# Weight chunks loaded in turns with batch 1, five shared buffers for k, q and v, and one compact copy, in a fused attention and MLP kernel

## The chip, the cores and the metric

The kernel runs on one core of one Trainium2 chip. The metric is the device time of one execution in microseconds (us); lower is better. A run of this one-core program is called slow when it is over 1.5% above the fastest run of the same kernel, and such runs are left out of ratios. The profile is one execution with the hardware profiler on; its span is a little shorter than the device time. All times inside a profile are counted from the start of its span.

Four engines matter here: TensorE (PE) multiplies matrices into the memory PSUM; ScalarE (ACT) and VectorE (DVE) empty PSUM, which is called an eviction; POOL and SyncE (SP) mostly issue DMA transfers. The granted clock is the share of its full speed that TensorE was given. A "dip" or "half clock" is a stretch of some 3.5 us in which it was near a half, so that four output matmuls take 1.90 us instead of 1.03.

## The reference, cut to what matters

```python
# q, k, v: (8 batches, 8 heads, 576 rows, 64); p: (8, 8, 32, 64)
p_packed = softmax(p @ k.T / 8) @ v            # 32 packed rows per head
attn     = softmax(q @ p_packed.T / 8) @ p_packed
x   = attn laid out as (8 * 576, 512)
h   = x @ w_in                                 # 512 -> 2048
g   = s * relu(h) ** 2 + b
out = g @ w_out                                # 2048 -> 512
```

## The kernel before

Everything is computed per batch. The packed values are first multiplied with W_in (`pw`, four chunks of 512 columns), so that a hidden block is the attention weights `aT` times `pw`, two by two matmuls of 288 columns. A block goes through a relu on ScalarE and a square on VectorE into `gT`; an output tile of 128 rows is then 16 "steps", one matmul with 128x512 of W_out each. `fill(n)` runs the next n output steps of the previous batch between other work, so that TensorE has something to do while ScalarE and VectorE empty PSUM.

Batches 0 to 2 transpose k and q on TensorE. From batch 3 on that is done by DMA from SyncE's queue: `dma_k` straight from the loaded k, `dma_q` from a copy of q re-laid by VectorE.

```python
def load(store, src, b, tag, h0=0, h1=H):          # POOL's queue, fp32 to bf16
    if h0 == 0:
        store[b] = rawp.tile([R, H, NC * D], BF16, tag=tag, name=tag)   # one buffer per tag
    pool.dma_start(out=store[b][:, h0:h1, :], in_=src[b, h0:h1]...)

for ch in range(NCH): load_w_in(ch)                # all of W_in, then all of W_out,
for m in range(0, NFF, 4): load_w_out(m, m + 4)    # then batch 1
load(kn, k, 1, "kn"); load(qn, q, 1, "qn"); load(vn, v, 1, "vn"); load_p(2, B)

def dma_k(b):                                      # SyncE's queue
    sp.dma_start_transpose(out=kT[b % 2]..., in_=kn[b]...)
def order_q(b):                                    # VectorE
    qr[b] = attp.tile(..., tag="qr", name="qr"); by_chunk(qr[b], qn[b])
def dma_q(b):                                      # SyncE's queue
    sp.dma_start_transpose(out=qT[b % 2]..., in_=qr[b]...)

# ... batches 0 and 1 by hand ...
second_scores(2); m1(1, 15)
todo = outs(1)                                     # five output tiles, 80 steps
packed_w1(2, 0); fill(6); weights(2, 0); fill(4); packed_w1(2, 1); weights(2, 1)
fill(6); packed_w1(2, 2); fill(4)
dma_k(3)

for b in range(2, B):                              # a = b + 1, c = b + 2
    # at block 1 (b == 2): packed_w1(2, 3), order_q(3), dma_q(3)
    # at block 3 + ...: first_scores(a), packed(a), second_scores(a) at block 9 (b == 2), ...
    # at block 4 (b == 2): loads(c)
    per = len(todo)
    for m in range(NFF):
        mlp_in(b, m)                               # one hidden block
        ... the steps of block m ...
        fill(per)
    fill(NFF * (NT + 1))
# [cut: the rest of the schedule]
```

The softmax here doesn't subtract the row's maximum and nothing guards it: scores larger than these inputs give would overflow.

Of the kernel before, what the change touches and what calls it, by code (L numbers as in the profile page):

```python
# [8 lines left out]
BF16 = mybir.dt.bfloat16  # L9
# [5 lines left out]
def kernel(  # L15
# [21 lines left out]
    B, H, S, D = q.shape  # L37
    NP = p.shape[2]
    DM = H * D
# [4 lines left out]
    R = 96  # L44
# [12 lines left out]

    constp = ctx.enter_context(tc.tile_pool(name="constp", bufs=1))
    wpool = ctx.enter_context(tc.tile_pool(name="wpool", bufs=1))
    rawp = ctx.enter_context(tc.tile_pool(name="rawp", bufs=1))  # L60
    attp = ctx.enter_context(tc.tile_pool(name="attp", bufs=1))
    atp = ctx.enter_context(tc.tile_pool(name="atp", bufs=2))
    smp = ctx.enter_context(tc.tile_pool(name="smp", bufs=2))
# [22 lines left out]
    def big(dt=F32):  # L86
        w = NB if dt == F32 else 2 * NB
        return psh.tile([P, 2, w], dt, tag="h", name="hps")


    kn, qn, vn = {}, {}, {}

    def load(store, src, b, tag, h0=0, h1=H):
        if h0 == 0:
            store[b] = rawp.tile([R, H, NC * D], BF16, tag=tag, name=tag)
        pool.dma_start(
            out=store[b][:, h0:h1, :],
            in_=src[b, h0:h1].rearrange("h (r c) d -> r h (c d)", c=NC),
        )
# [17 lines left out]
    def load_w_out(m0, m1):  # L117
        pool.dma_start(
            out=w_out_sb[:, m0:m1, :],
            in_=moe_w_out[m0 * P:m1 * P, :].rearrange("(m p) d -> p m d", p=P),  # L120
        )
# [17 lines left out]
    bvec = constp.tile([P, 1], F32, name="bvec")  # L139
    sp.dma_start(out=bvec[:], in_=moe_b[0:1].unsqueeze(0).to_broadcast([P, 1]))  # L140
    nc.scalar.preload_act_table_set("natural_log_exp_and_others")
    for ch in range(NCH):
        load_w_in(ch)
    for m in range(0, NFF, 4):
        load_w_out(m, m + 4)

    KW = H * HS + 32
    kT = [constp.tile([P, KW], BF16, name=f"kT{i}") for i in range(2)]
# [17 lines left out]
    def idle(n):  # L166

        t = big()
        for x in range(n):
            mm(t[:, 0, :], zeros[:, 0:P], zeros[:], start=True, stop=True)  # L170

    load(kn, k, 1, "kn")
    load(qn, q, 1, "qn")
    load(vn, v, 1, "vn")
    load_p(2, B)

# [24 lines left out]
    def prep_k(b, half):  # L201

        i = b % 2
        tp = big(BF16)
        for h4 in range(4):
            for cp in range(CP):
                tr(
                    tp[:, h4 // 2, (h4 % 2) * HS + cp * R:(h4 % 2) * HS + (cp + 1) * R],
                    kn[b][:, 4 * half + h4, cp * P:(cp + 1) * P],
                    identb[0:R, 0:R],  # L210
                )
        vec.tensor_copy(
            out=kT[i][:, half * 4 * HS:(half + 1) * 4 * HS].rearrange("p (a s) -> p a s", a=2),
            in_=tp[:, :, 0:2 * HS],
        )
# [5 lines left out]
        )  # L221

    def order_v(b):
        vr[b] = attp.tile([R, NC, HP, 2, D], BF16, tag="vr", name="vr")
        by_chunk(vr[b], vn[b])

    def order_q(b):
        qr[b] = attp.tile([R, NC, HP, 2, D], BF16, tag="qr", name="qr")
        by_chunk(qr[b], qn[b])

    def prep_q(b, half):

        i = b % 2
        tp = big(BF16)
        for x in range(2):
            hp = 2 * half + x
            for c in range(NC):
                for h2 in range(2):
                    tr(
                        tp[D * h2:D * h2 + D, x, c * R:(c + 1) * R],  # L240
                        qn[b][:, hp + HP * h2, c * D:(c + 1) * D],
                        identb[0:R, 0:R],
                    )
        for x in range(2):
            dst = qT[i][:, :, 2 * half + x, :]
            src = tp[:, x, 0:S].rearrange("p (c r) -> p c r", c=NC)
            if x == 0:
                act.copy(out=dst, in_=src)
            else:
                vec.tensor_copy(out=dst, in_=src)  # L250
# [34 lines left out]
    def packed(b, qd):  # L285
        i = b % 2
        if qd == 0:
            pps[b] = big()
        pp = pps[b]
        for hp in range(2 * qd, 2 * qd + 2):  # L290
            for c in range(NC):
                if b < N_PE_T:
                    for h2 in range(2):
                        o = hp * 2 * NP + h2 * NP
                        mm(
                            pp[D * h2:D * h2 + D, 0, o:o + NP],
                            vn[b][:, hp + HP * h2, c * D:(c + 1) * D],
                            e1[b][:, h2, c, hp, :],
                            start=(c == 0),
                            stop=(c == NC - 1),  # L300
                            tile_position=(0, D * h2),
                        )
                else:
                    mm(
                        pp[:, 0, hp * 2 * NP:(hp + 1) * 2 * NP],
                        vr[b][:, c, hp, :, :],
                        e1[b][:, :, c, hp, :],
                        start=(c == 0),
                        stop=(c == NC - 1),
                    )  # L310
        for c in range(NC):
            mm(
                pp[:, 1, qd:qd + 1],
                e1[b][:, qd, c, :, :],
                ones1[0:R, :],
                start=(c == 0),
                stop=(c == NC - 1),
            )
        if qd == NQ - 1:
            for h2 in range(2):  # L320
                vec.tensor_copy(
                    out=ppc[i][D * h2:D * h2 + D, :, :],
                    in_=pp[D * h2:D * h2 + D, 0, 0:HP * 2 * NP].rearrange("p (a j) -> p a j", a=HP)[
                        :, :, NP * h2:NP * h2 + NP
                    ],
                )
            rd[b] = smp.tile([P, NQ], F32, tag="rd", name="rd")
            vec.reciprocal(out=rd[b][:], in_=pp[:, 1, 0:NQ])
            rs[b] = smp.tile([P, NQ], F32, tag="rs", name="rs")
            vec.tensor_scalar_mul(out=rs[b][:], in0=rd[b][:], scalar1=scale)  # L330
# [63 lines left out]
    def packed_w1(b, ch, on_act=True):  # L394

        i = b % 2
        if ch == 0:
            pw[b] = ppw.tile([P, NQ, DFF], BF16, tag="pw", name="pw")
        t = big()
        packed_mm(i, ch, [t[:, qd, :] for qd in range(NQ)])  # L400
        dst = pw[b][:, :, ch * NB:(ch + 1) * NB]
        if on_act:
            act.activation(out=dst[:, 0], in_=t[:, 0, :], func=AF.Copy, scale=rd[b][:, 0:1])
        else:
            vec.tensor_scalar_mul(out=dst[:, 0], in0=t[:, 0, :], scalar1=rd[b][:, 0:1])
        vec.tensor_scalar_mul(out=dst[:, 1], in0=t[:, 1, :], scalar1=rd[b][:, 1:2])
# [33 lines left out]
    def bias_part(cps, m):  # L440
        mm(cps, onesb[:], w_out_sb[:, m, :], start=(m == 0), stop=(m == NFF - 1))
        if m == NFF - 1:
            vec.tensor_scalar_mul(out=biasrep[:], in0=cps, scalar1=bvec[:])
# [64 lines left out]
    def loads(b):  # L508
        load(kn, k, b, "kn")
        load(qn, q, b, "qn")  # L510
        load(vn, v, b, "vn")

    def m1(b, *ms):
        for m in ms:
            mlp_in(b, m)
# [20 lines left out]
    idle(3)  # L536
    weights(0, 0)
    weights(0, 1)
    packed_w1(0, 1, on_act=False)
    idle(6)  # L540
    m1(0, 0, 1, 2, 3)
    packed_w1(0, 2, on_act=False)
    m1(0, 4, 5, 6)

    todo = outs(0)
    first, second = todo[0], todo[1]
    bps = big()
    m = 7
    for m0 in range(0, NFF, 4):
        for x in range(m0, m0 + 4):  # L550
            bias_part(bps[:, 0, :], x)
        if m < NFF:
            m1(0, m)
        first.step(4)
        if m < NFF:
            m1(0, m + 1)
        second.step(4)
        if m < NFF:
            m1(0, m + 2)
        if m0 == 0:  # L560
            packed_w1(0, 3, on_act=False)
        m += 3
    loads(2)
    todo = todo[2:]

    def fill(n):
        run_outs(todo, n)

    prep_k(1, 0)
    prep_k(1, 1)  # L570
    fill(4)
    first_scores(1, 0)
    fill(4)
    first_scores(1, 1)
    fill(4)
    prep_q(1, 0)
    prep_q(1, 1)
    fill(4)
    packed(1, 0)
    packed(1, 1)  # L580
    twice_p(2, B)
    fill(5)
    packed_w1(1, 0)
    second_scores(1)
    fill(3)
    packed_w1(1, 1)
    weights(1, 0)
    fill(2)
    weights(1, 1)
    prep_p(2)  # L590
    fill(2)
    packed_w1(1, 2)
    prep_k(2, 0)
    m1(1, 0, 1)
    packed_w1(1, 3)
    m1(1, 2)
    prep_k(2, 1)
    m1(1, 3, 4)
    first_scores(2, 0)
    m1(1, 5, 6)  # L600
    fill(4)
    first_scores(2, 1)
    m1(1, 7, 8)
    prep_q(2, 0)
    prep_q(2, 1)
    m1(1, 9, 10)
    packed(2, 0)
    m1(1, 11)
    packed(2, 1)
    loads(3)  # L610
    m1(1, 12, 13, 14)
    second_scores(2)
    m1(1, 15)
    todo = outs(1)
    packed_w1(2, 0)
    fill(6)
    weights(2, 0)
    fill(4)
    packed_w1(2, 1)
    weights(2, 1)  # L620
    fill(6)
    packed_w1(2, 2)
    fill(4)
    dma_k(3)

    for b in range(2, B):
        a = b + 1
# [66 lines left out]
```

## Time and profile before

| what | value |
|---|---|
| device time, 3 runs | 270.11 us median (268.8 to 270.27) |
| span of the profile | 267.1 us |
| TensorE busy | 247.3 us, 93% |
| TensorE's longest wait | 2.07 us, for the transpose of batch 3's k |
| mean granted clock | 0.994 |

The prediction below shows the page, the waits and the timeline around that wait (start, duration, engine or queue, operation, with the idle time before and what ended it in brackets). Here is the timeline of SyncE's queue from 86 to 91 us (start, duration of the issue, queue, operation):

```profile
84.16 3.23 SPq L82 DMA_TRANSPOSE kT<-kn  x1
87.58 3.00 SPq L82 DMA_TRANSPOSE qT<-qr  x1
```

And POOL's timeline from 86 to 96 us, with what ended the idle time in brackets:

```profile
90.64 0.78 POOL L82 DMA_DIRECT2D kn<-in_k_dram  x1 [16.87 <-issue]
91.41 0.77 POOL L82 DMA_DIRECT2D qn<-in_q_dram  x1
92.17 0.77 POOL L82 DMA_DIRECT2D vn<-in_v_dram  x1
```

The reader is to see the order: batch 3's k transpose at 84.16, its q transpose at 87.58, and only then, from 90.64, the three loads of batch 4. The q transpose landed 5.0 us after its issue, at 92.6, 2.0 us after the first load was issued. Why the loads were that late: batch 4's k goes into the buffer from which batch 3's k transpose reads. The trace names no releaser for this one load (`issue`), but that transpose landed at 84.16 + 5.4 = 89.6 and the load was issued 1.1 us later; in the changed kernel the two times are 80.59 + 5.3 = 85.9 and 86.99, again 1.1 us apart; and the k loads of batches 5 and 6, at 113.25 and 134.19, wait for `DMA kT<-kn` by name.

### The profile page before, as it was taken

The page shows a single profiled execution, that of the slowest core. Times are in us where ns is not written, and L with a number is a line of the kernel's source. Part 1 is how long each engine was busy: PE and PEld are TensorE (multiplying, and loading weights), DVE is VectorE, ACT ScalarE, POOL GpSimd, SP SyncE. Part 2 cuts the span into 40 slices and gives each one's busy share as a digit, 9 for nine tenths or more (in the row PEclk, how much of TensorE's full clock was granted, in tenths as well). Part 3 has the DMA queues.
Part 4 walks back from the last instruction along what each step waited for, and adds up shares of the span by engine and source line. Part 5 has one row for each costly group of instructions (what it writes and reads, how often), then busy time and mean ns, then how long its engine had stood idle before and what let it go on. Part 6 is the DMA issues. An engine that isn't in the chain of part 4 may idle for free.

```text
span 267.1 us, 5619 instructions
## 1 busy us (share of the span) xinstructions
PE 247.3 (93%) x2312; PEld 139.5 (52%) x2348; DVE 146.4 (55%) x304; ACT 142.9 (53%) x217; POOL 29.3 (11%) x44
## 2 busy tenths in 40 slices
PE   7898899968989699899999999999999999999993
PEld 2544455636744365465556555665565555555441
DVE  2347456457657555765793459456944574444221
ACT  1337542387796347865855575548653773443000
POOL 8435001201100300030030012000000000000000
PEclk9999999999999799999999999999999999999999
DMA  7999999993893997699979869994731113111332
GB/s 75 198 202 206 206 203 164 145 194 37 131 143 75 157 201 151 115 150 235 169 94 182 203 128 164 140 212 79 134 87 42 39 42 81 39 39 42 79 79 79
DMA packets 54634, 34.32 MB, mean 128 GB/s; under 512 B 27472, under 2 KB 50000, under 8 KB 54608
## 3 DMA queue, kind: packets, MB, share of 16 engines
q0 software_dynamic: 25200, 18.61, 48.8%
q1 hardware_dynamic: 29408, 15.34, 26.6%
q8 instruction: 18, 0.29, 0.5%
q14 instruction: 8, 0.07, 0.1%
HBM read 37.23 MB, written 9.44 MB: 175 GB/s over the span
## 4 chain that ended last, share of the span: by engine, by line
PE 73%; DMA 11%; ACT 6%; DVE 4%; issue 3%; POOL 1%; DVEq 0%; POOLq 0%; ACTq 0%
PE yps L71 42%; PE hps L71 30%; DMA w_out_sb<-in_moe_w_out_dram 5%; DMA w_in_sb<-in_moe_w_in_dram 4%; ACT rlu L82 3%; DMA kT<-kn 2%; DVE pw L82 1%; PE hps L74 1%; ACT rcd L82 1%; ACT ld L82 1%; DVE ysb L82 1%; ACT pw L82 1%; DVE qr L82 1%; DVE gT L82 1%; POOL kn L82 1%
## 5 line engine op out<-in xcount | busy, mean ns | idle before, releaser
L71 PE MATMUL yps<-w_out_sb,gT 128*128 128x512 bf16 x544 | 138.1, 381 | 2.8 <-issue 1.6
L82 ACT ACTIVATE rlu<-hps 128x576 bf16<-128x576 f32 x128 | 82.4, 649 | 75.5 <-PE hps L71 68.0
L82 DVE TENSOR_TENSOR gT<-rlu 128x576 bf16<-128x576 bf16 x128 | 58.0, 456 | 73.0 <-ACT rlu L82 72.0
L71 PE MATMUL hps<-aT,pw 128*128 128x288 bf16 x512 | 83.3, 287 | 4.0 <-DVE pbd L82 1.7
L71 PEld LDWEIGHTS <-gT 128*128 128x128 bf16 x576 | 53.0, 98 | 50.5 <-issue 6.4
L71 PEld LDWEIGHTS <-pw 128*128 128x128 bf16 x512 | 49.5, 98 | 38.8 <-issue 5.1
L82 DVE SCALAR_TENSOR_TENSOR ysb<-yps,svec,biasrep 128x512 f32<-128x512 f32 x36 | 26.8, 747 | 14.3 <-PE yps L71 14.0
L82 DVE TENSOR_SCALAR pw<-hps,rd 128x512 bf16<-128x512 f32 (+1 forms) x26 | 24.4, 950 | 3.8 <-ACT pw L82 2.0
L82 ACT ACTIVATE e<-hps 96x768 bf16<-96x768 f32 x16 | 12.8, 802 | 15.7 <-PE hps L71 15.5
L82 ACT ACTIVATE pw<-hps,rd 128x1024 bf16<-128x1024 f32 (+1 forms) x18 | 16.6, 922 | 4.0 <-PE hps L71 3.9
L82 POOL DMA_DIRECT2D kn<-in_k_dram x9 | 6.9, 768 | 104.7 <-DMA kT<-kn 57.8
L82 DVE TENSOR_TENSOR aT<-e,rcd 128x576 bf16<-128x576 bf16 x16 | 12.1, 759 | 9.9 <-ACT rcd L82 9.9
L71 PE MATMUL hps<-w_in_sb,ppc 64*32 64x512 bf16 x256 | 12.3, 383 | 1.6 <-ACT e L82 0.4
L71 PE MATMUL hps<-zeros 128*128 128x512 bf16 x41 | 12.3, 427 | 1.4 <-DVE zeros L82 1.3
L82 ACT ACTIVATE e<-hps,rs 128x576 bf16<-128x576 f32 x16 | 10.9, 738 | 3.7 <-PE hps L71 3.7
L71 PE MATMUL hps<-pbd,kT 128*128 128x64 bf16 x192 | 8.9, 197 | 3.1 <-DMA kT<-kn 2.1
L82 ACT ACTIVATE rcd<-ld 128x576 f32<-128x576 f32 x16 | 10.9, 682 | 0.5
L71 PEld LDWEIGHTS <-kT 128*128 128x128 bf16 x192 | 8.1, 100 | 5.5 <-DMA kT<-kn 2.4
L82 ACT ACTIVATE ld<-hps 128x576 f32<-128x576 f32 x16 | 10.3, 643 | 0.9 <-PE hps L71 0.9
L71 PEld LDWEIGHTS <-ppc 64*32 64x32 bf16 x384 | 4.4, 89 | 10.4 <-issue 8.7
L82 POOL DMA_DIRECT2D qn<-in_q_dram x8 | 6.2, 775 | 13.5 <-PE hps L74 9.6
L71 PEld LDWEIGHTS <-zeros 128*128 128x128 bf16 x44 | 4.1, 106 | 6.3 <-issue 2.6
(45 smaller groups left out, 114.5 us busy)
## 6 DMA issues: line engine op xcount, KB each, us to landing
qn<-in_q_dram POOLq DMA_DIRECT2D x8, 576.0 KB, 10.8
vn<-in_v_dram POOLq DMA_DIRECT2D x8, 576.0 KB, 12.7
out_dram<-ysb SPq DMA_DIRECT2D x24, 192.0 KB, 2.3
kn<-in_k_dram POOLq DMA_DIRECT2D x7, 576.0 KB, 7.9
out_dram<-ysb SPq DMA_DIRECT2D x24, 128.0 KB, 2.5
w_in_sb<-in_moe_w_in_dram POOLq DMA_DIRECT2D x8, 256.0 KB, 12.9
w_out_sb<-in_moe_w_out_dram POOLq DMA_DIRECT2D x4, 512.0 KB, 13.4
out_dram<-ysb SPq DMA_DIRECT2D x24, 64.0 KB, 2.1
```

Source lines behind the costliest of these rows:

```text
L71: return tc.keep_in_program_order(nc.tensor.matmul(*a, **kw))
L74: return tc.keep_in_program_order(nc.tensor.transpose(*a, **kw))
L82: return lambda *a, **kw: tc.keep_in_program_order(f(*a, **kw))
```

## The change

The intent: W_in and W_out chunks load in turns with batch 1's tensors between them, so that output steps of batch 0 and the transposes of batch 1 can start while weights still arrive; freed filler is spread over batch 1; k, q, v and their re-laid copies share five rotating buffers, so that loads can be issued earlier; and the packed values leave PSUM in one copy of 128 partitions in place of two of 64.

```diff
-    rawp = ctx.enter_context(tc.tile_pool(name="rawp", bufs=1))
+    rawp = ctx.enter_context(tc.tile_pool(name="rawp", bufs=5))
+    def raw(name):
+        return rawp.tile([R, S // R * DM], BF16, tag="raw", name=name)[:]
... load(), order_q() and order_v() take their tile from raw() ...
-    for ch in range(NCH):
+    for ch in range(2):
         load_w_in(ch)
-    for m in range(0, NFF, 4):
-        load_w_out(m, m + 4)
+        load_w_out(4 * ch, 4 * ch + 4)
     load(kn, k, 1, "kn")
+    load_w_in(2)
+    load_w_out(8, 12)
     load(qn, q, 1, "qn")
+    load_w_in(3)
+    load_w_out(12, 16)
     load(vn, v, 1, "vn")
... packed(), b < N_PE_T: both halves of the heads into the same columns, then
+                vec.tensor_copy(out=ppc[i][:].rearrange("p a j -> p (a j)"), in_=pp[:, 0, 0:HP * NP])
... batch 0: six dummy matmuls (idle(6)) dropped; m1(0, ..) in turns with t0.step(2),
... t1.step(2), prep_k(1, ..), first_scores(1, ..), prep_q(1, ..); 16 fewer fills ...
... batch 1: fills of 5, 4, 3, 4 and then 2, 2, 2, 2, 2, 3, 3 between its blocks ...
+    m1(1, 14)
+    packed_w1(2, 0)
+    fill(2)
+    weights(2, 0)
+    dma_k(3)
     m1(1, 15)
     todo = outs(1)
-    packed_w1(2, 0)
-    fill(6)
-    weights(2, 0)
+    packed_w1(2, 1)
     fill(4)
-    packed_w1(2, 1)
     weights(2, 1)
     fill(6)
     packed_w1(2, 2)
     fill(4)
-    dma_k(3)
```

More of the change, by code (lines that the diff above doesn't have):

```diff
@@ L91 @@
     kn, qn, vn = {}, {}, {}
+    def raw(name):
+        return rawp.tile([R, S // R * DM], BF16, tag="raw", name=name)[:]
     def load(store, src, b, tag, h0=0, h1=H):
         if h0 == 0:
-            store[b] = rawp.tile([R, H, NC * D], BF16, tag=tag, name=tag)
+            store[b] = raw(tag).rearrange("r (h x) -> r h x", h=H)
         pool.dma_start(
@@ L223, in order_v @@
     def order_v(b):
-        vr[b] = attp.tile([R, NC, HP, 2, D], BF16, tag="vr", name="vr")
+        vr[b] = raw("vr").rearrange("r (c h x d) -> r c h x d", c=NC, h=HP, x=2)
         by_chunk(vr[b], vn[b])
     def order_q(b):
-        qr[b] = attp.tile([R, NC, HP, 2, D], BF16, tag="qr", name="qr")
+        qr[b] = raw("qr").rearrange("r (c h x d) -> r c h x d", c=NC, h=HP, x=2)
         by_chunk(qr[b], qn[b])
@@ L293, in packed @@
                     for h2 in range(2):
-                        o = hp * 2 * NP + h2 * NP
                         mm(
-                            pp[D * h2:D * h2 + D, 0, o:o + NP],
+                            pp[D * h2:D * h2 + D, 0, hp * NP:(hp + 1) * NP],
                             vn[b][:, hp + HP * h2, c * D:(c + 1) * D],
@@ L319, in packed @@
         if qd == NQ - 1:
-            for h2 in range(2):
-                vec.tensor_copy(
-                    out=ppc[i][D * h2:D * h2 + D, :, :],
-                    in_=pp[D * h2:D * h2 + D, 0, 0:HP * 2 * NP].rearrange("p (a j) -> p a j", a=HP)[
-                        :, :, NP * h2:NP * h2 + NP
-                    ],
-                )
+            if b < N_PE_T:
+                vec.tensor_copy(out=ppc[i][:].rearrange("p a j -> p (a j)"), in_=pp[:, 0, 0:HP * NP])
+            else:
+                for h2 in range(2):
+                    vec.tensor_copy(
+                        out=ppc[i][D * h2:D * h2 + D, :, :],
+                        in_=pp[D * h2:D * h2 + D, 0, 0:HP * 2 * NP].rearrange("p (a j) -> p a j", a=HP)[
+                            :, :, NP * h2:NP * h2 + NP
+                        ],
+                    )
             rd[b] = smp.tile([P, NQ], F32, tag="rd", name="rd")
@@ L538 @@
     weights(0, 1)
-    packed_w1(0, 1, on_act=False)
-    idle(6)
-    m1(0, 0, 1, 2, 3)
-    packed_w1(0, 2, on_act=False)
-    m1(0, 4, 5, 6)
-    todo = outs(0)
-    first, second = todo[0], todo[1]
-    bps = big()
-    m = 7
-    for m0 in range(0, NFF, 4):
-        for x in range(m0, m0 + 4):
-            bias_part(bps[:, 0, :], x)
-        if m < NFF:
-            m1(0, m)
-        first.step(4)
-        if m < NFF:
-            m1(0, m + 1)
-        second.step(4)
-        if m < NFF:
-            m1(0, m + 2)
-        if m0 == 0:
-            packed_w1(0, 3, on_act=False)
-        m += 3
-    loads(2)
+    todo = outs(0)
+    t0, t1 = todo[0], todo[1]
     todo = todo[2:]
@@ L567, in fill @@
         run_outs(todo, n)
+    m1(0, 0, 1)
+    packed_w1(0, 1, on_act=False)
+    m1(0, 2, 3)
+    t0.step(2)
+    m1(0, 4)
+    t0.step(2)
+    m1(0, 5)
+    t1.step(2)
+    m1(0, 6)
+    t1.step(2)
     prep_k(1, 0)
+    m1(0, 7)
+    t0.step(2)
     prep_k(1, 1)
-    fill(4)
+    t0.step(2)
     first_scores(1, 0)
-    fill(4)
+    t1.step(2)
+    packed_w1(0, 2, on_act=False)
+    t1.step(2)
     first_scores(1, 1)
-    fill(4)
+    m1(0, 8)
     prep_q(1, 0)
+    m1(0, 9)
     prep_q(1, 1)
-    fill(4)
+    m1(0, 10)
+    loads(2)
+    m1(0, 11)
+    t0.step(2)
+    packed_w1(0, 3, on_act=False)
+    t0.step(2)
+    m1(0, 12)
+    t1.step(2)
+    m1(0, 13)
+    t1.step(2)
+    m1(0, 14)
+    bps = big()
+    for m in range(NFF // 2):
+        bias_part(bps[:, 0, :], m)
+    m1(0, 15)
+    for m in range(NFF // 2, NFF):
+        bias_part(bps[:, 0, :], m)
+    t0.step(4)
+    t1.step(4)
     packed(1, 0)
@@ L584 @@
     second_scores(1)
-    fill(3)
+    fill(4)
     packed_w1(1, 1)
     weights(1, 0)
-    fill(2)
+    fill(3)
     weights(1, 1)
     prep_p(2)
-    fill(2)
+    fill(4)
     packed_w1(1, 2)
@@ L597 @@
     prep_k(2, 1)
-    m1(1, 3, 4)
+    m1(1, 3)
+    fill(2)
     first_scores(2, 0)
-    m1(1, 5, 6)
-    fill(4)
+    m1(1, 4, 5)
+    fill(2)
     first_scores(2, 1)
-    m1(1, 7, 8)
+    m1(1, 6, 7)
+    fill(2)
+    loads(3)
     prep_q(2, 0)
     prep_q(2, 1)
-    m1(1, 9, 10)
+    m1(1, 8)
+    fill(2)
+    m1(1, 9)
     packed(2, 0)
-    m1(1, 11)
+    m1(1, 10)
+    fill(2)
     packed(2, 1)
-    loads(3)
-    m1(1, 12, 13, 14)
+    m1(1, 11, 12)
+    fill(3)
     second_scores(2)
+    m1(1, 13)
+    fill(3)
+    m1(1, 14)
+    packed_w1(2, 0)
+    fill(2)
+    weights(2, 0)
+    dma_k(3)
     m1(1, 15)
     todo = outs(1)
-    packed_w1(2, 0)
-    fill(6)
-    weights(2, 0)
+    packed_w1(2, 1)
     fill(4)
-    packed_w1(2, 1)
     weights(2, 1)
```

## The prediction

> **What bounds the kernel now.** I read the page first (busy shares, slices, the chain that ended last), then the waits of TensorE, then the timelines of TensorE, VectorE, ScalarE and the queues over the first 95 us, because the loop for batch 2 and later is touched by the diff only at its entry.
>
> From the page: the engine shares, four rows of the 40 slices (6.68 us each) and the chain.
>
> ```profile
> PE 247.3 (93%) x2312; PEld 139.5 (52%) x2348; DVE 146.4 (55%) x304; ACT 142.9 (53%) x217; POOL 29.3 (11%) x44
> ...
> PE   7898899968989699899999999999999999999993
> ...
> PEclk9999999999999799999999999999999999999999
> DMA  7999999993893997699979869994731113111332
> GB/s 75 198 202 206 206 203 164 145 194 37 131 143 75 157 201 151 115 150 235 169 94 182 203 128 164 140 212 79 134 87 42 39 42 81 39 39 42 79 79 79
> ...
> PE 73%; DMA 11%; ACT 6%; DVE 4%; issue 3%; POOL 1%; DVEq 0%; POOLq 0%; ACTq 0%
> ```
>
> TensorE is the bound: 247.3 of 267.1 us, and 73% of the chain. Its holes all lie in the first 14 slices, and there the DMA row is full: the load stream runs at 198 to 206 GB/s for the first 40 us. Slice 14 holds the only dip of the granted clock. So anything to win lies before about 95 us.
>
> The longest entries of TensorE's waits over the whole run:
>
> ```profile
> PE hps L71 <- DMA kT<-kn: 2.1, 1, 2.1
> PE hps L71 <- ACT rlu L82: 1.9, 6, 0.4
> PE hps L71 <- DVE pbd L82: 1.7, 2, 1.3
> ...
> PE hps L71 <- DMA w_out_sb<-in_moe_w_out_dram: 0.8, 1, 0.8
> ```
>
> TensorE's timeline around the first of them, and the SyncE queue at the same time:
>
> ```profile
> 86.83 0.65 PE L71 MATMUL hps<-aT,pw 128*128 128x288 bf16 x4
> 89.56 0.57 PE L71 MATMUL hps<-pbd,kT 128*128 128x64 bf16 x12 [2.07 <-DMA kT<-kn]
> 89.94 1.90 PE L71 MATMUL yps<-w_out_sb,gT 128*128 128x512 bf16 x4
> 91.62 1.17 PE L71 MATMUL hps<-aT,pw 128*128 128x288 bf16 x4
> ```
> ```profile
> 44.19 39.86 SPq L82 DMA_DIRECT2D out_dram<-ysb  x10
> 84.16 3.23 SPq L82 DMA_TRANSPOSE kT<-kn  x1
> ```
>
> Two things to see. The transpose of batch 3's k stands behind ten output stores in SyncE's order, the last two of which wait for the first output tile of batch 1, so it starts at 84.16 although k was requested at 63.18; it lands 5.4 us later. And after the 2.07 us hole the same four-matmul group takes 1.90 us instead of the usual 1.03: the clock is halved. The windows view of 89.56 to 93.40 gives a mean granted clock of 0.56, so 3.84 x 0.44 = 1.7 us are lost on top of the 2.1.
>
> **What the Trainium skill says.** "TensorE: Matmul & The Clock Gate", Part 1, says that an idle window of about 3.4 us puts TensorE at half clock, and that the window runs freely. The trace agrees on the half clock and on its length (about 3.5 us), but here 2.07 us of idling was enough. The same page's closing table advises no idle gaps over about 3 us; I take 2 us as already risky. "DMA: Bandwidth & Descriptors", Queues, rings and completion order, says that each DMA engine consumes a ring in order; so a load queued later on one queue lands later. The trace agrees: batch 1's k, q and v, issued 22.41, 24.48 and 25.27, took 16.7, 17.5 and 19.6 us, that is they landed at 39.1, 42.0 and 44.9, one 576 KB tensor every 2.9 us (about 200 KB/us). "VectorE: DVE Perf Modes", Why tensor_reduce can't reduce along partition axis, says each partition is its own lane; so a copy of 128 partitions should cost what one of 64 costs with the same row length, 286 ns by the group of the ppc casts.
>
> **The change, part by part.**
>
> *Transpose of k earlier.* In the changed SyncE order it stands behind eight stores, not ten: only batch 0's four tiles. I expect those done near 76 us, the transpose to start near 77 and land near 83, against a need near 88. Both the 2.1 us wait and the 1.7 us of half clock vanish: **3.8 us gained**. The five shared buffers make batch 3's k load earlier still, since its slot is batch 1's q, free after its transposes near 38. Before, it waited for batch 2's own k. In the steady loop the five slots rotate onto the same reuse distances as before, so nothing changes there.
>
> *Load order.* I lay the same bytes on the 200 KB/us line through the measured landings (v of batch 0 at 14.4, first W_out chunk at 28.5 after 4352 KB). Now: W_out chunk 0 at 20.7, W_in 1 at 23.7, k at 28.8, W_in 2 at 31.4, q at 36.8, W_in 3 at 39.4, W_out 3 at 42.0, v at 44.8. Nothing gets shorter; the order alone changes.
>
> *First stage on TensorE, from 23.16* (second half of the first hidden block, held by the ScalarE Ln/Exp chain in both kernels, so the six dropped dummy matmuls save nothing) *to the end of batch 1's packing.* Unit costs from pitches in the timeline: hidden block 0.49, output step 0.216, packed W_in chunk 0.34, k transposes 0.57 a half, q 0.55 a half, scores 0.35, packing 0.65, bias row 0.216. Before: 26.6 us of work in 23.16 to 51.97, 2.2 of stalls. After: 16 output steps move out (3.45 us), so about 23.4 of work. But I walk through the new order and find waits: about 0.5 before block 4 and 0.6 before block 8, as the two VectorE evictions of a packed chunk take 1.40 us together and are now asked for just in time; 0.4 for a gT; then q: TensorE gets to its transposes at 35.1, q lands at 36.8, **1.7 lost**; 0.2 for a buffer, 1.2 around packed chunk 3, 0.4 of small ones. Sum **5.0**, so stalls grow by 2.8.
>
> *Second stage, the softmax chain of batch 1* (51.97 to 59.97 before: 8.0 us, 5.1 of work, 2.9 idle). Its length is set by ScalarE's e, Ln, Exp. The fills go 5, 4, 3, 4 where 12 steps ran: 4 more hide 0.86 us. The finished third tile puts a 0.75 us eviction in front of a packed eviction on VectorE, which gives most of that back: stalls 2.7, gain 0.2. The compact copy (one of 0.29 for two, 0.61) is hidden behind fill(5), 1.08 us, here and behind idle(5) for batch 0: gain 0 to 0.3.
>
> *Third stage, 59.97 to 76.17*: 14.1 us of work in 16.2, so 2.1 of stalls, mostly relu evictions of hidden blocks in a row (relu 0.65 against 0.49). Now 16 steps are spread in twos and threes where 4 stood in one lump. They should cover all but 0.6: **1.5 gained**.
>
> Sum: 3.8 - 2.8 + 0.2 + 1.5 = 2.7 us. From that I take 0.6 for the clock: with the dummies gone TensorE has nearly 3 us of holes around 20 to 23 us, and the q wait is 1.7 us; either may halve the clock. The first is absorbed by the q wait, the second would cost about 1.2, taken half. Net about 2.1 to 2.4 us.
>
> **The rivals.**
>
> *A: q isn't late, or the evictions overlap better than I walked.* The floor after q at 36.8 is 13.1 us of work, to 49.9 instead of my 51.6, and the second stage may keep its 0.9. For it: the new order looks arranged around these loads. Against: the landing line is measured to a few tenths. Gain then about 5.5 us, 264.6.
>
> *B: half clock takes the place.* Two or three dips in the first 60 us instead of one at 90, each worth up to 1.7 us. For it: a 2.07 us hole did it once. Against: the early drop falls into waiting time. Time 269 to 271.
>
> *C: the transpose was not the real bound, and what follows it in batch 2 waits for something else,* for instance the transpose of q, issued at 87.58 and wanted near 101. There are some 6 us of slack, so I give this little weight. Gain near zero, 270.
>
> **Range and chances.** 270.1 - 2.4 gives 267.7. The sure part is 3.8 us; the stages before it can return all of that (B, 270.7) or only a third of what I charge (A, 264.5). Two per cent faster is 264.7, the edge of A; 2% slower would need 5 us of new stalls beyond those charged.
>
> **What would show it.** Right: no wait for kT near 88 and full clock in that slice; kT's transpose starting between 73 and 80; a wait of 1 to 2.5 us for q before batch 1's q transposes, near 36; packing of batch 1 ending near 51.6; fewer relu waits between 60 and 77; ppc copies of about 290 ns at 128 partitions. Wrong: no q wait, a clock dip after it, or a new long wait inside batch 2.

## The result, and the profile after

The changed kernel took 277.26 us (median of 4 runs, 276.68 to 279.08) against 269.46 us for the kernel before (4 runs). The ratio is 1.030, 95% interval 1.0238 to 1.0361: 3% slower, outside the predicted range and on the other side. A ratio here is the mean time of one kernel's fast runs over that of the other's of the same rounds, so it isn't quite the ratio of the medians that are quoted. All runs of both were fast ones; the profiled one had a mean granted clock of 0.972.

From the page after, the same rows as the prediction shows of before:

```profile
PE 253.6 (92%) x2342; PEld 140.7 (51%) x2342; DVE 146.4 (53%) x301; ACT 143.4 (52%) x217; POOL 29.6 (11%) x44
...
PE   6875999979999977879999999999999999999993
...
PEclk9997999997999997979999999999999999999998
DMA  7999999995145994699869976993671112211222
...
PE 66%; DMA 16%; ACT 8%; DVE 5%; issue 2%; POOL 1%; POOLq 0%; DVEq 0%; ACTq 0%
```

TensorE is busy 6.3 us longer although it has six matmuls less to do. Part of that is only records (of the 576 matmuls of the output steps, the trace of before has 544, the one after all); the clock row shows where the rest comes from. There are four dips (slices 4, 10, 16 and 18; 6.9 us each) where there was one. DMA's share of the chain rose from 11 to 16%. TensorE's longest waits:

```profile
PE hps L71 <- DMA qT<-qr: 4.0, 2, 3.5
PE hps L71 <- DVE aT L82: 2.9, 2, 2.0
PE hps L71 <- ACT rlu L82: 1.5, 3, 0.7
```

The wait for kT is gone. In its place stands a wait for qT, the transpose of q: 3.54 us at one place and 0.46 at another. TensorE's timeline from 101 to 110.2 us:

```profile
105.33 0.44 PE L71 MATMUL hps<-qT,ppc 64*32 64x288 bf16 x16 [3.54 <-DMA qT<-qr]
105.71 1.52 PE L71 MATMUL yps<-w_out_sb,gT 128*128 128x512 bf16 x5
107.02 1.17 PE L71 MATMUL hps<-aT,pw 128*128 128x288 bf16 x4
107.98 2.23 PE L71 MATMUL yps<-w_out_sb,gT 128*128 128x512 bf16 x5
```

The five output steps after the wait take up to 2.23 us where five take 1.24 at full clock. And the same two queues as above, SyncE's from 80 to 96 us and then POOL's:

```profile
80.59 3.94 SPq L82 DMA_TRANSPOSE kT<-kn  x1
86.82 1.12 SPq L82 DMA_DIRECT2D out_dram<-ysb  x2
89.66 5.24 SPq L82 DMA_TRANSPOSE qT<-qr  x1
```
```profile
86.99 0.78 POOL L82 DMA_DIRECT2D kn<-in_k_dram  x1 [21.56 <-issue]
89.81 0.77 POOL L82 DMA_DIRECT2D qn<-in_q_dram  x1 [2.04 <-DVE qr L82]
91.72 0.77 POOL L82 DMA_DIRECT2D vn<-in_v_dram  x1 [1.15 <-DVE vr L82]
```

The order is turned around. Batch 4's k now goes 2.67 us ahead of batch 3's q transpose, and its q and v go alongside. The q transpose landed 15.5 us after its issue, at 105.2, against 5.0 us before. The chain of that stretch (84 to 125 us) gives 37.9% of its length to this one transfer.

The second loss stands at the end of batch 2's blocks, timeline from 116 to 124 us:

```profile
117.28 0.37 PE L71 MATMUL hps<-w_in_sb,ppc 64*32 64x512 bf16 x1 [0.60 <-ACT rlu L82]
117.82 0.62 PE L71 MATMUL hps<-w_in_sb,ppc 64*32 64x512 bf16 x15 [0.17 <-ACT rlu L82]
119.66 0.65 PE L71 MATMUL hps<-aT,pw 128*128 128x288 bf16 x4 [1.22 <-ACT pw L82]
120.15 0.78 PE L71 MATMUL hps<-pbd,kT 128*128 128x64 bf16 x12
120.74 1.90 PE L71 MATMUL yps<-w_out_sb,gT 128*128 128x512 bf16 x4
```

There are no output steps between these: batch 2's loop took five per block (its list still held five unfinished tiles, as only 14 steps had run before it), and but for a single step in block 13 they ran out after block 12. Blocks 13 to 15 then stand bare behind ScalarE, and a dip of the clock follows.

Laid side by side at points that both traces have (start of the matmuls named, us; "evened" corrects for output steps done earlier or later than in the other kernel, at 0.216 us each):

| point | before | after | lag | evened |
|---|---|---|---|---|
| block 0 of batch 1 | 59.97 | 59.93 | 0.0 | +3.4 (16 steps behind) |
| block 0 of batch 2 | 82.22 | 84.29 | +2.1 | +3.4 (6 behind) |
| second scores of batch 3, less the 3.54 us wait | 101.14 | 101.79 | +0.6 | 0.0 (3 ahead) |
| the same, with the wait | 101.14 | 105.33 | +4.2 | +3.5 |
| first scores of batch 4 | 113.64 | 120.15 | +6.5 | +6.5 |
| end of the span | 267.1 | 275.8 | +8.7 | +8.7 |

So the early k transpose did give back all that the first stages had lost, 3.4 us. Everything after that is loss: 3.5 us of wait for q's transpose; 3.0 us up to batch 4's first scores, namely 1.7 of half clock (4.80 us at 0.64 in the windows view of 105.3 to 110.1) and 2.2 of waits at the end of the blocks, where before had 1.0; and 2.2 us after it, of which 1.7 are the dip from 119.6 to 124 (4.40 us at 0.61) and 0.46 the second wait for a q transpose.

### The profile page after: what moved, and what is told of

Read it like the earlier page. It is cut to its first block, busy times and chain, and to the rows that moved or that the text cites. A ratio compares the mean times of both kernels' runs of the same rounds, so it can differ in the third digit from the quotient of the medians.

```text
span 275.8 us, 5640 instructions
## 1 busy us (share of the span) xinstructions
PE 253.6 (92%) x2342; PEld 140.7 (51%) x2342; DVE 146.4 (53%) x301; ACT 143.4 (52%) x217; POOL 29.6 (11%) x44
## 4 chain that ended last, share of the span: by engine, by line
PE 66%; DMA 16%; ACT 8%; DVE 5%; issue 2%; POOL 1%; POOLq 0%; DVEq 0%; ACTq 0%
PE yps L71 36%; PE hps L71 29%; DMA qT<-qr 12%; DMA vn<-in_v_dram 4%; ACT rlu L82 3%; ACT rcd L82 2%; ACT ld L82 2%; DVE pw L82 1%; PE hps L74 1%; ACT pw L82 1%; DVE aT L82 1%; DVE qr L82 1%; ACT e L82 1%; DVE gT L82 1%; POOL kn L82 1%
## 5 line engine op out<-in xcount | busy, mean ns | idle before, releaser
L71 PE MATMUL yps<-w_out_sb,gT 128*128 128x512 bf16 x576 | 147.3, 385 | 0.2
L71 PE MATMUL hps<-aT,pw 128*128 128x288 bf16 x512 | 86.4, 294 | 7.1 <-DVE aT L82 2.9
L71 PEld LDWEIGHTS <-gT 128*128 128x128 bf16 x576 | 53.6, 99 | 51.9 <-issue 7.4
L71 PE MATMUL hps<-zeros 128*128 128x512 bf16 x38 | 10.8, 423 | 1.9 <-DVE zeros L82 1.3
L82 ACT ACTIVATE rcd<-ld 128x576 f32<-128x576 f32 x16 | 10.9, 683 | 0.5
L82 POOL DMA_DIRECT2D vn<-in_v_dram x8 | 6.2, 775 | 32.5 <-PE hps L71 12.0
```

The lines of the kernel that those rows point to most:

```text
L71: return tc.keep_in_program_order(nc.tensor.matmul(*a, **kw))
L82: return lambda *a, **kw: tc.keep_in_program_order(f(*a, **kw))
```

## The experiments

Fifteen experiments ran, of thirteen kernels (two were run twice), all correct. Each ran on one chip, with runs of the kernel before among them; ratios are against those. Ratios are compared below only with their intervals in view.

### Batch 4's loads held until batch 3's q transpose has landed

```diff
+    def gate(b):
+        pool.tensor_copy(out=gatev[:], in_=qT[b % 2][:, 0, 0, 0:1])   # POOL waits for qT
-            at(1 + d, lambda: loads(c))
+            at(1 + d, lambda: (gate(a), loads(c)) if b == 2 else loads(c))
```

> The changed kernel, with batch 4's three loads held back on the POOL queue until batch 3's q transpose has landed. Theory (the loads of batch 4, released early by the early k transpose, share the DMA engines with the q transpose and stretch it from about 7.5 to 15.6 us): the q transpose lands within 8 us of its issue at about 89.7, the 3.5 us wait before batch 3's second scores and the half clock after it (1.9) vanish, and the time falls from 277 to about 272. Rival (the q transpose is late because its source copy on VectorE is late, or is slow by itself after the stores): it still lands near 105 and the time stays at 277. Second rival: held back, the loads make batch 4's own k transpose late and the time is given back there.

Measured: 270.09 us against 268.09, ratio 1.0099 (1.0063 to 1.0134); 5.4 us off the changed kernel's 1.030 (0.0201 x 268; the intervals are far apart). POOL's timeline:

```profile
93.70 0.19 POOL L82 COPY gatev<-qT 128x1 bf16<-128x1 bf16 x1 [29.05 <-DMA qT<-qr]
94.82 0.78 POOL L82 DMA_DIRECT2D kn<-in_k_dram  x1 [0.93 <-issue]
```

The q transpose, issued at 88.89, landed in 4.7 us in place of 15.5, with the same source and the same two stores ahead of it. The first rival doesn't hold: the transpose isn't slow by itself. Nor does the second in this run: batch 4's k transpose, now from a k loaded 8 us later, made no new wait. Where TensorE got there earlier, it did hold in part. In the later runs with held loads that k transpose took 7.6 to 10.6 us to land, against 5.4 to 6.5 for the k transposes of the kernel before, and TensorE waited 0.43 and 0.57 us for it in two of them and 1.32 us in a third. The held loads take their place beside the next transpose. The 5.4 us agree with the wait of 3.5 and the 1.7 of half clock behind it.

### Four output steps per block in batch 2

```diff
-        per = len(todo)
+        per = 4 if b == 2 else len(todo)
```

> The changed kernel, with four output steps per hidden block in batch 2's loop (as the kernel before had) where it has five. Theory (with five, the steps run out after block 12, so the last blocks, batch 3's packed W_in and scores stand bare behind ScalarE's evictions: 2.2 us of waits, then 1.7 us of half clock near 120): those waits shrink below 1 us, no clock dip near 120, time 277 falls to about 273.5. Rival (those waits are the late second scores of batch 3 handed on, not missing filler): they stay and the time stays within 1 us of 277.

Measured: 276.06 us, ratio 1.0351 (1.0282 to 1.042), no gain. But the trace isn't that of the rival: the waits of 0.60 and 1.22 us near the end of the blocks are gone, only 0.42 is left there, and there is no dip near 120. What took their place, from TensorE's timeline:

```profile
105.36 0.68 PE L71 MATMUL hps<-qT,ppc 64*32 64x288 bf16 x16 [5.78 <-DMA qT<-qr]
```

With fewer steps before it TensorE comes to q's transpose earlier, at 99.6, and waits there until the same 105.4. By the time alone the rival's number came true, by the trace its reason didn't. My expectation missed that the two losses lie in series: mending the later one alone is paid for by the earlier one.

### The early k transpose alone, in the kernel before

```diff
     second_scores(2)
+    dma_k(3)
     m1(1, 15)
...
     fill(4)
-    dma_k(3)
```

> The kernel before with the transpose of batch 3's k alone moved ahead of block 15 of batch 1. Prediction's account: the 2.1 us wait and 1.7 us of half clock vanish, 3.8 us faster than before (about 266). New theory: k lands earlier, its buffer is free earlier, batch 4's loads start ahead of batch 3's q transpose as in the changed kernel, and the wait comes back at batch 3's second scores: no faster than before, perhaps 1 to 2 us slower (269 to 272).

Measured: 266.10 us, ratio 0.9937 (0.9896 to 0.9977), and one of four runs at 274.5, which counts as slow. My new theory was wrong on the time and right on the release. Batch 4's k did go early, at 78.55 by POOL's timeline, so far ahead of q's transpose (87.09) that it was through; only batch 4's q and v (87.24 and 89.16) met it. It took 10.8 us, landed at 97.9 and was wanted at 98.03. So the early transpose does gain, 1.7 us by the ratio instead of 3.8; that the kernel before doesn't pay the half clock in each run (below) fits this, but wasn't tested by itself. Where the 274.5 came from no trace shows.

### The k transpose put back, in the changed kernel

```diff
     weights(2, 0)
-    dma_k(3)
...
     fill(4)
+    dma_k(3)
```

> The changed kernel with the transpose of batch 3's k put back behind the last fill before batch 2's loop. Theory of the early release: the q transpose again goes ahead of batch 4's loads and lands in 8 to 10 us, so the 3.5 us wait there vanishes, but the 2 us wait for k with its half clock may come back: about 273 to 275. Rival (the early k transpose has nothing to do with the loss): 279 to 281, the loss of the changed kernel plus the 3.8 us of the k wait.

Measured: 276.79 us, ratio 1.0314 (1.0241 to 1.0387); the profiled run was a slow one, at 281.19. The experiment didn't do what it was made for. The k transpose started at 82.86 instead of 80.59, but this run was 3.2 us late already at batch 1's packing (53.70 against 50.51), so by its place in the work the transpose isn't later at all: with only 14 steps run by then no store of batch 1's first tile stood in front of it in SyncE's order, and batch 4's k still went at 89.21, ahead of q's transpose at 91.93. What the order of the queue in this one slow run suggests is that in the changed kernel the missing stores, more than the place of the line `dma_k(3)`, moved the transpose forward. The early release is tested by the held loads, not by this run.

### Both mends

The two edits above (held loads, four steps) together.

> The changed kernel with both mends: batch 4's loads held until batch 3's q transpose has landed, and four output steps per block in batch 2's loop. The first gave 0.020 of the ratio (1.030 to 1.010), the second nothing by itself, since TensorE came to the late q transpose sooner (wait 5.8 instead of 3.5 us) and its own waits near 117 to 120 did vanish. Theory (two losses in series, the first hides the second's mend): now no wait for q's transpose, no 1.2 us wait on the packed eviction, at most one clock dip, and 3.5 to 4 us off the first mend's run: ratio 0.994 to 0.999. Rival (the second loss is worth nothing): ratio stays near 1.010.

Measured: 270.10 us against 268.10, ratio 1.0054 (1.0006 to 1.0103). The wait for q's transpose, the 1.22 us wait and the dips at 107 and 121 are all gone in its trace. The gain over the first mend is 0.0045, or 1.2 us, less than the 3.5 to 4 I expected, and the intervals of the two runs overlap, so the times don't show it. The page showed two dips left, near 24 and 62 us. The same kernel run again gave 1.0018 (below), still short of the 0.994 to 0.999 expected.

### The early k transpose and the held loads, in the kernel before

> The kernel before with the early k transpose and batch 4's loads held until batch 3's q transpose has landed. Early k alone gave 0.9937 in its fast runs, with the q transpose landing 10.8 us after its issue, 0.1 us ahead of its use, and one of four runs at 274.5. Theory: the q transpose now lands within 8 us, with some 3 us to spare; ratio 0.990 to 0.995 and no run above 269. If the changed kernel's load order and its other block order are worth anything by themselves, the run with both mends beats this one; I expect this one to win by 0 to 1 us.

Measured: 266.66 us against 268.10 of the same chip, ratio 0.9938 (0.9894 to 0.9982), six runs from 265.99 to 267.29. The q transpose landed in 4.7 us. It beat the run with both mends by 3.4 us, where I had expected 0 to 1. Holding the loads adds nothing to the ratio of the early transpose alone, as TensorE wasn't waiting; the outlier didn't return in six runs, which is too few to say that holding cured it.

### q re-laid and transposed early, in the changed kernel

```diff
     weights(2, 0)
     dma_k(3)
+    order_q(3)
+    dma_q(3)
-            at(1, lambda: (packed_w1(2, 3), order_q(3), dma_q(3)))
+            at(1, lambda: packed_w1(2, 3))
```

(with four steps per block; the loads aren't held)

> The changed kernel with batch 3's q re-laid and transposed right behind its k transpose, ahead of batch 1's last block, instead of in batch 2's second block; four steps per block; the loads aren't held. Another remedy for the same cause: the q transpose starts about 3 to 8 us sooner, so even stretched to 12 to 16 us by batch 4's loads it lands before its use near 99. Theory: no wait at batch 3's second scores, ratio 0.994 to 1.000, as with the loads held. If it lands late all the same, the queue to the DMA engines is the limit, not the order.

Measured: 268.46 us, ratio 1.0018 (0.9966 to 1.0071). Issued at 84.34, the q transpose took 10.9 us, landed at 95.2, and was wanted at 99.54: no wait there. A wait of 1.71 us for the next batch's q transpose came up instead, at 124.25. Two loads met it (batch 4's k, issued at 83.20, and its q at 88.52; v came at 95.79). It agrees with the theory by another remedy: give the transpose its slot, or give it time. The ratio came out just above the expected 0.994 to 1.000.

### The parts by themselves

Five shared buffers alone, in the kernel before:

> The kernel before with only its k, q, v, re-laid q and v put into five shared rotating buffers; loads, steps and copies as before. Theory: batch 3's k is loaded earlier (near 50 instead of 63) but its transpose stays behind the ten stores at 84, and batch 4's k still waits for that transpose to land, so nothing moves on TensorE: ratio 0.995 to 1.005. Rival (the shared rotation itself ties loads to wrong releases and costs time): ratio above 1.01, with new waits of POOL on the loads that TensorE or the transposes feel.

Measured: 269.07 us, ratio 1.0036 (0.9974 to 1.0099): the same. The k transpose started at 84.05 as before. One part of the theory failed: batch 4's k didn't wait for that transpose to land (89.5), but was issued at 87.96, 0.5 us behind q's transpose. That one then took 9.2 us instead of 5.0 and landed at 96.7, 2.7 us before its use at 99.4. So the shared buffers can let a load go early too; here there was time for it. This run's trace is of use for another reason. It has the 2.1 us wait for kT, and after it:

```profile
89.47 0.52 PE L71 MATMUL hps<-pbd,kT 128*128 128x64 bf16 x12 [2.10 <-DMA kT<-kn]
89.83 1.03 PE L71 MATMUL yps<-w_out_sb,gT 128*128 128x512 bf16 x4
```

The same hole as in the kernel before, without half clock: 1.03 us for the four steps, not 1.90. So a hole of 2 us doesn't always halve the clock.

Buffers of their own in the changed kernel (the five shared ones taken back):

> The changed kernel with the five shared buffers taken back to five of their own, as in the kernel before; everything else of the change kept. Theory (the loads of batch 4 are let loose by the early landing of the k transpose, and by the re-laying of q and v, with either set of buffers): POOL still issues batch 4's loads around batch 3's q transpose, that transpose still takes 13 to 16 us, ratio stays 1.025 to 1.035. Rival (the shared rotation lets the loads go early): the loads start later, the wait for q's transpose goes, ratio 1.00 to 1.012.

Measured: 277.83 us, ratio 1.0352 (1.0298 to 1.0406), with the q transpose at 15.6 us and POOL issuing batch 4's loads at 87.09, 89.73 and 91.65, within 0.1 us of the changed kernel. So the shared buffers aren't the cause of the changed kernel's loss. They do what they were meant to (batch 2's q is issued at 34.45 with them and at 39.09 without), but nothing on TensorE waited for it.

The compact copy alone, in the kernel before (edit as in the change):

> The kernel before with the one compact copy of the packed values alone (one copy of 128 partitions in place of two of 64, for batches 0 to 2). Prediction: one copy of about 0.29 us in place of 0.61, hidden behind dummies or output steps in batches 0 and 1, some 0.2 us in batch 2; ratio 0.997 to 1.001.

Measured: 268.58 us, ratio 1.0007 (0.9956 to 1.0057): the same. In the changed kernel's trace the copy of 128 partitions takes 0.29 us.

### What was left: the clock in the first 70 us

The six dummies back, on top of both mends:

```diff
     weights(0, 0)
     weights(0, 1)
+    idle(6)
```

> The changed kernel with both mends (ratio 1.0054) and the six dummy matmuls put back where TensorE waits for the first softmax weights, near 20 us. Prediction's account: the half clock seen in most runs from 24 to 28 us is gone, but the time stays, as batch 1's q lands near 37 either way and TensorE waits for it longer: ratio 1.003 to 1.008. Rival (the early half clock does cost): 1.5 us less, ratio 0.998 to 1.001.

Measured: 267.99 us against 268.10, ratio 0.9987 (0.9946 to 1.0029): the time fits the rival. But the run without the dummies was of another call, and the two intervals overlap. The six runs' mean clocks are 0.992 to 1.000, without the dummies 0.984 to 0.994.

The third tile of batch 0 finished later, on top of both mends without the dummies:

```diff
     prep_p(2)
-    fill(4)
+    fill(3)
     packed_w1(1, 2)
...
     m1(1, 3)
-    fill(2)
+    fill(3)
     first_scores(2, 0)
```

> The changed kernel with both mends, and the third output tile of batch 0 finished a few blocks later (fills of 5, 4, 3, 3 and a fill of 3 after block 3 of batch 1), so that its eviction no longer stands in front of a packed W_in eviction on VectorE near 60 us. Prediction's account: that eviction costs 0.7 us and leads to the half clock seen near 62: the wait before block 1 of batch 1 falls from 0.74 to near 0, the clock dips there less often, ratio 0.998 to 1.003 against 1.0054. Rival: the wait moves on to the next block and the ratio stays at 1.005.

Measured: 268.69 us, ratio 0.9997 (0.995 to 1.0043). The reading on TensorE is plain. The changed kernel, timeline from 59.5 to 64.5 us:

```profile
59.93 0.66 PE L71 MATMUL hps<-aT,pw 128*128 128x288 bf16 x4 [1.18 <-DVE pbd L82]
61.33 0.65 PE L71 MATMUL hps<-aT,pw 128*128 128x288 bf16 x4 [0.74 <-ACT rlu L82]
61.91 0.42 PE L71 MATMUL hps<-w_in_sb,ppc 64*32 64x512 bf16 x8
62.26 1.14 PE L71 MATMUL hps<-aT,pw 128*128 128x288 bf16 x4
```

and with the late tile, 50 to 90 us:

```profile
59.96 1.43 PE L71 MATMUL hps<-aT,pw 128*128 128x288 bf16 x8 [1.34 <-DVE pbd L82]
61.36 0.41 PE L71 MATMUL hps<-w_in_sb,ppc 64*32 64x512 bf16 x8
61.70 0.66 PE L71 MATMUL hps<-aT,pw 128*128 128x288 bf16 x4
```

Blocks 0 and 1 go through in one piece, the 0.74 us wait is gone, and no half clock follows (a block of four matmuls at 0.66, not 1.14).

All four mends together, then the two runs beside it for comparison on the same chip:

> The changed kernel with all four mends: loads held, four steps, the six dummies back, the third tile late. If the dummies' 0.0067 and the late tile's 0.0057 of the ratio add up: 0.992 to 0.995, as good as the kernel before with the early k transpose (0.9938). If both only remove the same clock dips by chance of phase: 0.997 to 1.000.

> The run with both fixes once more, on the chip of the run with all mends. If dropping the dummies costs (half clock in the first 30 us, not all of it hidden by the wait for q): ratio again 1.003 to 1.008, mean granted clock below 0.99, above the fully mended kernel by 1.5 us or more. If the first result was a matter of chips: 0.997 to 1.001.

> The kernel before with the early k transpose and the loads held, once more, beside the fully mended changed kernel. Expected 0.991 to 0.996 again, and within 0.4% of the fully mended one: the change's load order and block order then win nothing beyond the early k transpose.

Measured, against 268.65 us of the kernel before on that chip:

| kernel | median us | ratio (95%) | mean clock of the six runs |
|---|---|---|---|
| changed, all four mends | 267.00 | 0.9931 (0.9891 to 0.9971) | 0.997 to 1.000 |
| changed, the two mends | 269.80 | 1.0018 (0.997 to 1.0065) | 0.983 to 0.987 |
| before, early k transpose, loads held | 266.49 | 0.9913 (0.9872 to 0.9955) | 0.994 to 0.999 |

The fully mended kernel came out where I expected it (0.992 to 0.995), and its clock is near full in all six runs. Together the dummies and the late tile are worth 2.8 us, and the six runs of each don't overlap (266.55 to 267.99 against 268.07 to 270.18). What each is worth alone isn't shown: the run with two mends repeated at 1.0018 instead of 1.0054, between my two expectations for it, and against that the single mends (0.9987 and 0.9997) are within the intervals.

The profiles of these two runs say where their 3.4 us of span went. TensorE comes to batch 1's q with no wait and with 1.14 us of it, and starts it at 36.96 and 36.52, so the early dip is nearly all hidden there, as the prediction had it. At the second scores of batch 3 the lag has grown from 0.4 to 1.9 us (100.25 against 98.30), with the dip near 62 in between; at the first scores of batch 4 it is 3.4 (114.75 against 111.32), and 1.32 of that is a wait for batch 4's k transpose, which took 10.5 us beside the held loads. So in this pair the late dip and the slowed transpose account for most of it. One profile shows one run, and how often the wait comes, no run shows.

The best kernel is the one before with the early k transpose and the held loads, some 0.6 to 0.9% faster than before. It is shown faster by the interval, but not by 2%. The change's new load order, once mended, is within 0.2% of it, so no run shows that it gains anything beyond the early k transpose.

## Why the prediction was wrong

**The bound.** That TensorE is the bound holds. Two readings of the page were loose: the DMA row isn't full over the first 14 slices (slices 10 and 13 are at 3), and TensorE's row has an 8 in slice 17 as well. There, from 107 to 114 us, lie the 1.0 us of waits at the end of batch 2's blocks, the place where the second loss grew. The sentence that failed is the one that set the scope: "the loop for batch 2 and later is touched by the diff only at its entry", and with it "so nothing changes there" in the buffer part. Batch 2's loop got a new entry state in two ways, and both losses of the result lie in it.

**The transpose of k earlier: right in itself.** It started at 80.59, 3.6 us later than the 77 expected, landed at 85.9, and there is no wait for kT. The point by point gain of 3.4 us from block 0 of batch 2 to the second scores of batch 3 is the 3.8 predicted, within what one trace tells. In the kernel before it is worth 1.7 us by the ratio of 0.9937 (0.0063 x 268) and 3.1 by the two spans (267.1 to 264.0). Probably the half clock that I added in full comes in some runs only: of the kernel before's eleven runs in one call, clocks reach from 0.983 to 1.000 and times from 266.89 to 270.11.

**The step that failed: the slack of q's transpose. Rival C is where it went, and I gave it little weight.** The prediction named the transpose of q as the next thing that could be waited for and set its slack at some 6 us (by the landing in the trace of before, 92.6, and its use at 101.14 it was 8.5). It did not ask what the early k would release. The slack was a measurement of a queue without loads in front: batch 4's k waits for the k transpose that reads its buffer, so moving that transpose forward moved the loads forward, past q's transpose, which stayed tied to its copy on VectorE in block 1. 5.0 us became 15.5, the transpose was issued 2.1 us later and wanted 0.6 later, so the 8.5 of slack became a wait of 3.5, and 1.7 of half clock followed. The held loads (4.7 us, no wait, 5.4 us back), the early q transpose (no wait at 99.5) and the buffers of their own (no difference) show this cause and clear the shared buffers. Between 4.7 and 15.5 lie the runs in which the transpose met fewer loads, or the first of them later: 9.2 us (five buffers), 10.8 (early k transpose in the kernel before), 10.9 (q early).

"DMA: Bandwidth & Descriptors", Queues, rings and completion order, of the Trainium skill says that each DMA engine takes turns between the queue rows that have work, a packet at a time. Loads are on POOL's row and transposes on SyncE's, so neither should block the other; the measured 15.5 against 4.7 us says that sharing cost the transpose a factor of three, and it landed (105.2) with the last of the three loads (91.72 + 14.3 = 106.0). That it is the turn taking that does this, no run here shows.

**A second step that the prediction lacks: the count of steps.** I moved output steps between stages and never carried the count into the loop. 14 instead of 20 before it leave the first tile unfinished, so the loop takes five per block, and runs dry after block 12: 2.2 us of waits and a dip. With four steps these waits and the dip are gone from the traces. Its worth in time is less sure: alone it shows nothing (ratio 1.0351), since it lies behind the wait for q, and on top of the held loads it gave 1.0099 to 1.0054, within the intervals, and 1.0018 in the repeat.

**The first stage: right, within 0.4 us.** Packing of batch 1 predicted to end at 51.6, measured 52.0; q predicted to land at 36.8, TensorE begins its transposes at 36.98. Of the 1.7 us wait for q only traces hold little (0.2 in the changed kernel, 1.16 with the late tile), as half clock from 24 to 28 us brought TensorE there later: the prediction's "absorbed by the q wait". So the end came right with the dip where the wait was to be.

**The second stage: right.** The softmax chain took 7.9 us (8.0 before, 7.8 predicted). The third tile's eviction did cost the 0.7 us, though behind the chain, in front of block 1.

**The third stage: wrong.** "All but 0.6: 1.5 gained" didn't come. With no dip in it (the run with held loads), TensorE waits 3.0 us in the waits view of 59.5 to 83.5, and 3.0 in the corresponding stretch before. The fills did take away the short waits of 63 to 76 us, but the 0.74 us behind the third tile's eviction and one of 0.47 near 79.5 came up. The late tile's run removes the former.

**The clock: mis-sized.** I took 0.6 us for it. Four dips of 1.7 us each (windows view: 4.00 us at 0.58, 3.60 at 0.53, 4.80 at 0.64, 4.40 at 0.61) stand against one before; the first is hidden, the other three cost 5.1 us. Rival B had the kind right and its places in part: two of the four lie near the first 60 us, the other two come after the new waits in batch 2.

**Compact copy and shared buffers: right on the time**, 0.29 us as read from the 64-partition casts, and no effect on the time of either alone. That nothing else changes with the shared buffers isn't so: alone they let batch 4's k go ahead of its old release (above).

## What to carry to other kernels

When a transfer is moved forward, list what waits for its end, and ask with whom the released transfers will then share the queues: the slack of the next transfer in line, measured with the queues empty, doesn't hold any more. When filler is moved between stages, carry the count to the end of the last loop that uses it. And mend losses that stand in series together, or the first one will make the second look worthless.

## What the Trainium skill lacked or had wrong

- "TensorE: Matmul & The Clock Gate", Part 1, gives half clock after an idle window of about 3.4 us, and the page's closing table advises against gaps over about 3 us. Here a hole of 2.07 us was followed by half clock for some 3.5 us in the kernel before, and the same hole (2.10 us) in the run with five buffers by none; a 1.18 and a 0.74 us hole 0.7 us apart were followed by it too. That the same hole counts in one run and not in another agrees with a window that runs freely, as the page has it; that 2.07 us can be enough doesn't agree with 3 us as a safe limit.
- "DMA: Bandwidth & Descriptors", Latency and other measured facts, gives the bandwidth of a DMA transpose as 261 GB/s in one kernel and some 350 to 400 where the data is contiguous. No page gives a figure for what loads on another queue do to it. Here one transpose of the same 576 KB took 4.6 to 5.0 us to land with the engines nearly to itself and 15.5 with three loads of 576 KB around it.
- No page says that releases chain across queues in this way (transpose ends, its source buffer goes free, a load starts, the next transpose is slowed). The number is the 5.4 us that holding the loads gave back.
